# Block decay factors by two small DMAs per block in place of ones-products on TensorE, with a new plan of the instruction order

## The chip, the cores and the metric

The kernel runs on one core of a Trainium2 chip. The metric is the device time of one execution in microseconds (us), the median of several runs. Engines: PE is TensorE (PEld its weight loads), DVE VectorE, ACT ScalarE, POOL GpSimd, SP SyncE, whose queue issues nearly all DMAs here. Lines such as L412 are lines of the kernel that the profile belongs to, so the same function has another number in each kernel.

## The reference

A gated linear attention over 4 x 8 sequences of 768 steps with head size 48, then an MLP with squared rectifier on the 3072 tokens (384 to 2048 to 384):

```python
for t in range(S):
    state = alpha[:, :, t, :, None] * state + np.einsum('bhd,bhe->bhde', k[:, :, t], v[:, :, t])
    y[:, :, t] = np.einsum('bhd,bhde->bhe', q[:, :, t], state)
...
h = x @ w_in
r = np.maximum(h, 0.0)
g = s * (r * r) + b
return g @ w_out
```

`alpha` lies between 0.8 and 1. The kernel cuts the tokens into 24 blocks of 128 (six per batch entry, all heads together). In a block, `b` is the exponential of the running sum of log alpha, the queries are multiplied by `b` and the keys by `1/b`. The state passed to the next block is multiplied by `b` at the block's last step, one factor per head and channel: the *block decay*. The state has channels in partitions, while `b` has time in partitions, so the decay must get from one row (partition 127) into a column.

## The kernel before

The kernel plans itself. Each step is registered with its engine, an assumed duration, a priority and what it reads and writes; a list scheduler then fixes the order of instructions on every engine. On an engine, the ready step with the lowest priority number goes first. SP is planned as an engine too, and executes its queue strictly in that order.

```python
def st_cum(n):                       # PE: running sum, and the sum over the whole block as a column
    la = la_sb[n % 2]
    nc.tensor.matmul(out=cum_ps, lhsT=U_bf, rhs=la[:, :, 0:D], start=True, stop=True)
    if n % NCH == NCH - 1:
        return
    laf = la.rearrange("a h d -> a (h d)")
    for p in range(NP):              # the four ones-products
        nc.tensor.matmul(out=bl_ps[:, p : p + 1], lhsT=laf[:, 128 * p : 128 * p + 128],
                         rhs=ones_col_bf, start=True, stop=True)

def st_exp_b(n):
    nc.scalar.activation(out=b_sb[n % 2], in_=cum_ps, func=AF.Exp)

def st_exp_i(n):
    nc.scalar.activation(out=binv_sb[n % 2], in_=cum_ps, func=AF.Exp, scale=-1.0)
    if n % NCH != NCH - 1:
        nc.scalar.activation(out=blast_sb[n % 2], in_=bl_ps, func=AF.Exp)

def st_snew(n):                      # POOL: new state = (old state + product) * decay
    if n % NCH in (0, NCH - 1):
        return
    bl = blast_sb[n % 2].unsqueeze(2).to_broadcast([128, NP, 96])
    nc.gpsimd.tensor_tensor(out=s_sb[n % 3], in0=t1_sb[n % 2], in1=bl, op=ALU.mult)
# ... cut: for the first block of a sequence st_t1 applies the decay on DVE

def load_op(x, n):                   # the input loads of block n, on SP
    op("SP", TB, loads.index(f"{x}{n}") - 1000, load, n, *SRC[x], w=[(x, n % NIN)], lat=2.0)
```

Five input buffers per operand (`NIN = 5`) let loads run ahead. Blocks 0 to 3 are done in pairs by other code, which the change hardly touches.

## Time and profile before

| | before |
|---|---|
| median of the first three runs | 189.17 us (186.81 to 189.44) |
| span of the profiled core, granted clock | 183.4 us, 1.0 |
| PE / DVE / ACT / POOL busy | 95 / 76 / 58 / 22 % |
| PE from 60 to 180 us | 120.00 us busy of 120 |
| decay ones-products | 64 matmuls (four in each of 16 blocks) |

Busy shares are shares of the whole span.

### The profile page before, as it was taken

To read this page: it belongs to the slowest core of one execution; us is meant where nothing else is said; L and a number is where in the kernel's file an instruction comes from. 1 tells how busy PE (TensorE), PEld (TensorE's weight loads), DVE (VectorE), ACT (ScalarE), POOL (GpSimd) and SP (SyncE) were. 2 spreads that over 40 slices of the span, in tenths; PEclk is the share of its full clock that TensorE was granted. 3 is DMA by queue.
4 is the path that set the end of the run, shared out by engine and by line. 5 is a ranking of instruction groups with operands and counts; after the bars stand their busy time and mean duration, and the time that the engine had idled before them with its cause. 6 is when DMAs were issued, how large, how long until landed. Compare 5 with 4: busy or idle time off the path is not lost.

```text
span 183.4 us, 5324 instructions
## 1 busy us (share of the span) xinstructions
PE 174.6 (95%) x2133; PEld 124.2 (68%) x2135; DVE 138.7 (76%) x255; ACT 106.0 (58%) x215; POOL 40.2 (22%) x70
## 2 busy tenths in 40 slices
PE   6988896999999999999999999999999999999993
PEld 2356574767777776676776776776876776777762
DVE  2377999999899898687789688577897788544421
ACT  3437699946676565674764754853753662665400
POOL 7995032022112423110303311101230131000000
PEclk9999999999999999999999999999999999999999
DMA  5999999999999999996998979996974994101112
GB/s 154 355 295 321 361 370 323 193 178 223 201 185 199 214 183 192 205 211 156 228 169 178 211 153 215 185 228 146 210 175 103 209 194 119 46 4 43 43 43 86
DMA packets 115816, 34.42 MB, mean 188 GB/s; under 512 B 109008, under 2 KB 114256, under 8 KB 115792
## 3 DMA queue, kind: packets, MB, share of 16 engines
q1 hardware_dynamic: 98832, 29.89, 69.2%
q10 hardware_dynamic: 16896, 4.20, 15.7%
q8 instruction: 16, 0.26, 0.6%
q14 instruction: 8, 0.07, 0.1%
q0 software_dynamic: 64, 0.00, 0.0%
HBM read 25.17 MB, written 4.72 MB: 163 GB/s over the span
## 4 chain that ended last, share of the span: by engine, by line
PE 79%; DVE 8%; SPq 6%; DMA 4%; issue 1%; DVEq 0%
PE o_ps L754 32%; PE h_ps L692 31%; PE py_ps L527 5%; SPq L217 5%; PE a_ps L489 4%; DMA gt<-in_k_dram 4%; PE ct_ps L386 2%; DVE colpart L342 2%; DVE gt L707 1%; SPq L309 1%; PE ct_ps L447 1%; PE ct_ps L433 1%; DVE colsum L347 1%; DVE qk L589 1%; PE o_ps L723 1%
## 5 line engine op out<-in xcount | busy, mean ns | idle before, releaser
L692 PE MATMUL h_ps<-xd,w_in_bf 128*128 128x256 bf16 (+1 forms) x624 | 74.4, 265 | 0.1
L701 ACT ACTIVATE r<-h_ps 128x512 bf16<-128x512 f32 x96 | 56.3, 604 | 30.3 <-PE h_ps L692 22.8
L754 PE MATMUL o_ps<-w_out_bf,gt 128*128 128x384 bf16 x368 | 69.5, 326 | 1.4 <-ACT w_out_bf L318 1.3
L692 PEld LDWEIGHTS <-w_in_bf 128*128 128x128 bf16 x624 | 55.1, 97 | 11.1 <-issue 0.4
L707 DVE TENSOR_TENSOR gt<-r 128x512 bf16<-128x512 bf16 x96 | 42.7, 456 | 19.5 <-ACT r L701 18.4
L754 PEld LDWEIGHTS <-gt 128*128 128x128 bf16 x368 | 34.6, 98 | 19.4 <-issue 1.5
L498 DVE TENSOR_TENSOR am<-a_ps,mask 128x1024 bf16<-128x1024 f32 x24 | 29.3, 1221 | 2.3 <-PE a_ps L489 2.0
L483 POOL TENSOR_TENSOR s_st<-s_st,blast 128x384 bf16<-128x384 bf16 x16 | 14.6, 914 | 63.7 <-DVE s_st L472 46.0
L410 POOL CAST vp<-v_in 128x384 bf16<-128x384 f32 x20 | 12.2, 608 | 47.7 <-DMA v_in<-in_v_dram 40.7
L672 ACT ACTIVATE xd<-py_ps 128x384 bf16<-128x384 f32 x22 | 11.0, 502 | 17.8 <-PE py_ps L527 15.9
L765 DVE SCALAR_TENSOR_TENSOR o_sb<-o_ps,s_col,bias_w 128x384 f32<-128x384 f32 x23 | 14.2, 616 | 6.0 <-PE o_ps L754 5.0
L380 ACT ACTIVATE la<-a_in 128x384 bf16<-128x384 f32 x20 | 10.4, 521 | 7.3 <-DVE gt L707 4.5
L416 DVE TENSOR_TENSOR qk<-q_in,b_s 128x384 bf16<-128x384 f32 x20 | 12.5, 627 | 0.8 <-ACT b_s L402 0.7
L421 DVE TENSOR_TENSOR qk<-k_in,binv 128x384 bf16<-128x384 f32 x20 | 11.9, 596 | 0.1
L402 ACT ACTIVATE b_s<-ct_ps 128x384 f32<-128x384 f32 x20 | 9.7, 486 | 2.6 <-PE ct_ps L386 2.2
L405 ACT ACTIVATE binv<-ct_ps 128x384 f32<-128x384 f32 x20 | 9.9, 495 | 0.0
L489 PE MATMUL a_ps<-qkT 64*128 64x128 bf16 x192 | 9.5, 219 | 0.4 <-DVE am L498 0.2
L489 PEld LDWEIGHTS <-qkT 64*128 64x128 bf16 x192 | 5.5, 94 | 6.5 <-issue 5.1
L1026 PE MATMUL o_ps<-zeros 128*128 128x512 bf16 x19 | 7.7, 551 | 1.3 <-DVE zeros L235 1.3
L527 PE MATMUL py_ps<-am,vp 128*32 128x128 bf16 x352 | 8.8, 219 | 0.0
L472 DVE TENSOR_TENSOR s_st<-ct_ps,s_st 64x192 bf16<-64x192 f32 x20 | 7.0, 352 | 2.0 <-PE ct_ps L447 1.6
L527 PEld LDWEIGHTS <-vp 128*32 128x32 bf16 x384 | 6.5, 97 | 0.9 <-issue 0.6
(95 smaller groups left out, 133.4 us busy)
## 6 DMA issues: line engine op xcount, KB each, us to landing
out_dram<-o_sb SPq DMA_DIRECT2D x23, 192.0 KB, 2.5
v_in<-in_v_dram SPq DMA_DIRECT2D x20, 192.0 KB, 3.8
a_in<-in_alpha_dram SPq DMA_DIRECT2D x20, 192.0 KB, 4.1
k_in<-in_k_dram SPq DMA_DIRECT2D x20, 192.0 KB, 4.0
q_in<-in_q_dram SPq DMA_DIRECT2D x20, 192.0 KB, 3.9
wst<-in_moe_w_in_dram SPq DMA_DIRECT2D x4, 768.0 KB, 7.5
gt<-in_moe_w_out_dram SPq DMA_DIRECT2D x4, 768.0 KB, 9.2
gt<-in_alpha_dram SPq DMA_DIRECT2D x2, 384.0 KB, 4.9
```

Of the source, the lines that this page charges most:

```text
L410: nc.gpsimd.tensor_copy(out=vp_sb[n % 4].rearrange("a p (x d) -> a p x d", d=D)[:, :, 0:3:2, :], in_=v_in[n % NIN].rearrange("a (p e) d -> ...
L416: nc.vector.tensor_tensor(out=qk_sb[n % 4][:, 0, :, 0:D], in0=q_in[n % NIN], in1=b_sb[n % 2], op=ALU.mult)
L421: nc.vector.tensor_tensor(out=qk_sb[n % 4][:, 1, :, 0:D], in0=k_in[n % NIN], in1=binv_sb[n % 2], op=ALU.mult,)
L483: nc.gpsimd.tensor_tensor(out=s_sb[n % 3], in0=t1_sb[n % 2], in1=bl, op=ALU.mult)
L489: nc.tensor.matmul(out=a_ps[:, e, p, :], lhsT=qkT[64 * e : 64 * e + 64, 1, p, :], rhs=qkT[64 * e : 64 * e + 64, 0, p, :], start=True, stop ...
L498: nc.vector.tensor_tensor(out=am_sb[n % 2].rearrange("a e p t -> a (e p) t"), in0=a_ps.rearrange("a e p t -> a (e p) t"), in1=(mask2 if n ...
L527: nc.tensor.matmul(out=y_of(n)[32 * (x % 4) : 32 * (x % 4) + 32, x // 4, :], lhsT=(st[:, p, c0 : c0 + 32] if e is None else vp[:, p, c0 + ...
L692: nc.tensor.matmul(out=hp[:, i * n : (i + 1) * n], lhsT=w_in_bf[:, kk, 128 * j : 128 * (j + 1)], rhs=xd_sb[g % 3][:, kk, 0:n], start=(kk = ...
L701: nc.scalar.activation(out=r_sb[w % 2], in_=h_ps[w % 2], func=AF.Relu)
L707: nc.vector.tensor_tensor(out=gt_sb[:, s0 : s0 + m, js[0] : js[0] + len(js)].rearrange("a s j t -> a j s t"), in0=r, in1=r, op=ALU.mult,)
L754: nc.tensor.matmul(out=op[:, 0:d_model], lhsT=gt_sb[:, s0, j], rhs=w_out_bf[:, j, :], start=(j == 0), stop=(j == NJ - 1),)
L765: nc.vector.scalar_tensor_tensor(out=ots, in0=o_ps[(x // 4) % 2][:, 0:d_model], scalar=s_col, in1=bias_w, op0=ALU.mult, op1=ALU.add,)
```

## The change

Intent: take the four ones-products and their small exponential out of every block from the ninth on. The exponential `b` is written so that its last row holds, for each half, the four values of a channel side by side (16 bytes), and two DMAs of 768 bytes spread that row over 48 partitions each. The core of the diff (cut, among others: a new load order, the new values of `P` and of other planning numbers, the wider `blast`, the product that reads `b`, and the plan of the pairs):

```diff
-GROUPS = [2, 2, 1, 1, 2, 2, 2, 2, 2, 2, 2, 2, 2]
+GROUPS = [2, 1, 1, 1, 2, 1, 2, 2, 2, 2, 2, 2, 1, 1, 1, 1]
-NPE = 8
-NAY = 12
+NPE = 9
+NAY = 10
+NBL = 8
+TBL = 0.5
+BLP = -2072
-VC2 = ["ACT", "ACT"]
+VC2 = ["DVE", "DVE"]
 ...
-        if n % NCH == NCH - 1:
+        if n % NCH == NCH - 1 or n >= NBL:
             return
 ...
+    def st_bl(n):
+        row = b_edp(n)[C - 1 : C]
+        for e in range(2):
+            nc.sync.dma_start(
+                out=blast_all[64 * e : 64 * e + D, n % 4, :], in_=row[:, e]
+            )
+
+    def b_edp(n):
+        return b_all[:, n % 2].rearrange("a h d -> a (h d)").rearrange(
+            "a (e d p) -> a e d p", e=2, p=NP
+        )
+
+    def b_of(n):
+        if n < NBL or last_chunk(n):
+            return b_sb[n % 2]
+        return b_edp(n).rearrange("a e d p -> a p e d")
 ...
     def st_exp_b(n):
-        nc.scalar.activation(out=b_sb[n % 2], in_=cum_ps, func=AF.Exp)
+        nc.scalar.activation(out=b_of(n), in_=cum_of(n), func=AF.Exp)
 ...
+            op("ACT", 0.41, t + P["ei"], st_exp_i, n, r=["ct"], w=[("bi", i2)])
+            if not last(n):
+                op("SP", TBL, BLP, st_bl, n, r=[("b", i2)], w=[("bl", s4)], lat=2.0)
```

More of the change, by code (lines that the diff above doesn't have):

```diff
@@ L16 @@
 VW = 144
-GROUPS = [2, 2, 1, 1, 2, 2, 2, 2, 2, 2, 2, 2, 2]
-UNIT = 0.548
-LEAD = {1: 116.8, 2: 316.2, 4: 55.7}
-NPE = 8
-NAY = 12
+GROUPS = [2, 1, 1, 1, 2, 1, 2, 2, 2, 2, 2, 2, 1, 1, 1, 1]
+UNIT = 0.987
+LEAD = {1: 120.0, 2: 301.2, 4: 39.8}
+NPE = 9
+NAY = 10
 RING = 12
@@ L34 @@
 NY = 2
-NKV = 9
+NKV = 8
 NR2 = 2
+NBL = 8
+TBL = 0.5
+BLP = -2072
 TC2 = ["DVE", "DVE"]
-VC2 = ["ACT", "ACT"]
+VC2 = ["DVE", "DVE"]
 CE = ["POOL", "DVE", "ACT", "ACT", "ACT", "ACT", "ACT", "ACT"]
@@ L42 @@
 COLD = 9.0
-P_BM, P_CS, P_BMM = -5, -166.6, 420.9
+P_BM, P_CS, P_BMM = -5, -184.4, 500.0
 P = dict(
-    ln=37.38, cum=-5.89, eb=-21.67, ei=-20.73, vc=52.19, qb=-9.21, kb=4.29, T=47.45,
-    Tc=-10.24, KV=-8.06, t1=-26.76, sn=121.36, Ay=-20.23, A=-31.59, mk=-31.84, y=-27.08,
-    ye=22.77, m1=-10.34, re=8.62, sq=-6.75, m2=-16.59, oe=-37.4, vm=-45.28, ci=-71.74,
-    co=-1313.2, ls=295.04, vn=18.84,
+    ln=30.89, cum=6.75, eb=-15.73, ei=-37.64, vc=58.22, qb=-18.21, kb=1.37, T=51.05,
+    Tc=-26.12, KV=1.1, t1=-18.5, sn=118.41, Ay=-23.07, A=-38.42, mk=-38.49, y=-33.32,
+    ye=38.86, m1=-17.0, re=-0.58, sq=-13.12, m2=-10.9, oe=-38.9, vm=-33.56, ci=-135.11,
+    co=-1083.2, ls=80.19, vn=-135.38,
 )
-LOADS = ["V0", "i0", "A0", "K0", "Q0", "A1", "V1", "Q1", "i1", "K1", "i2", "i3", "v4", "o0", "o1", "o2", "o3", "a4", "k4", "q4"]
+LOADS = ["A0", "V0", "i0", "V1", "A1", "o0", "Q0", "K0", "i1", "K1", "Q1", "i2", "o1", "i3", "v4", "a4", "q4", "o2", "o3", "k4"]
 class Schedule:
@@ L288 @@
     am_sb = many("am", 2, [128, 2, NP, 128], BF16)
-    blast_all = sb.tile([128, 2, NP], BF16, name="blast")
-    blast_sb = [blast_all[:, i] for i in range(2)]
+    blast_all = sb.tile([128, 4, NP], FP32, name="blast")
+    nc.vector.memset(blast_all, 1.0)
+    blast_sb = [blast_all[:, i] for i in range(4)]
     xd_sb = many("xd", 3, [128, 3, 512], BF16)
@@ L399, in st_cum, with last_chunk, cum_of @@
             )
+    def last_chunk(n):
+        return n % NCH == NCH - 1
+    def cum_of(n):
+        return cum_ps if n < NBL or last_chunk(n) else by_pair(cum_ps)
     def st_exp_b(n):
-        nc.scalar.activation(out=b_sb[n % 2], in_=cum_ps, func=AF.Exp)
+        nc.scalar.activation(out=b_of(n), in_=cum_of(n), func=AF.Exp)
     def st_exp_i(n):
         nc.scalar.activation(out=binv_sb[n % 2], in_=cum_ps, func=AF.Exp, scale=-1.0)
-        if n % NCH != NCH - 1:
-            nc.scalar.activation(out=blast_sb[n % 2], in_=bl_ps, func=AF.Exp)
+        if n % NCH != NCH - 1 and n < NBL:
+            nc.scalar.activation(out=blast_sb[n % 4], in_=bl_ps, func=AF.Exp)
+    def st_bl(n):
[12 more added lines that the diff above has]
+        return b_edp(n).rearrange("a e d p -> a p e d")
     def st_vcast(n):
@@ L413, in st_vcast, with by_pair @@
         )
+    def by_pair(x):
+        return x.rearrange("a (p e) d -> a p e d", e=2)
     def st_qb(n):
-        nc.vector.tensor_tensor(
-            out=qk_sb[n % 4][:, 0, :, 0:D], in0=q_in[n % NIN], in1=b_sb[n % 2], op=ALU.mult
-        )
+        out, in0 = qk_sb[n % 4][:, 0, :, 0:D], q_in[n % NIN]
+        b = b_of(n)
+        if len(b.shape) == 4:
+            out, in0 = by_pair(out), by_pair(in0)
+        nc.vector.tensor_tensor(out=out, in0=in0, in1=b, op=ALU.mult)
     def st_kb(n):
@@ L463, in st_t1 @@
     def st_t1(n):
-        bl = blast_sb[n % 2].unsqueeze(2).to_broadcast([128, NP, D])
+        bl = blast_sb[n % 4].unsqueeze(2).to_broadcast([128, NP, D])
         for e in range(2):
@@ L481, in st_snew @@
             return
-        bl = blast_sb[n % 2].unsqueeze(2).to_broadcast([128, NP, 96])
+        bl = blast_sb[n % 4].unsqueeze(2).to_broadcast([128, NP, 96])
         nc.gpsimd.tensor_tensor(out=s_sb[n % 3], in0=t1_sb[n % 2], in1=bl, op=ALU.mult)
@@ L584, in pair_exp_i @@
         )
-        nc.scalar.activation(out=blast_all, in_=bl2_ps, func=AF.Exp)
+        nc.scalar.activation(out=blast_all[:, 2 * m % 4 : 2 * m % 4 + 2], in_=bl2_ps, func=AF.Exp)
     def pair_mul(m, x):
@@ L879, in add_block @@
         op("ACT", 0.45, t + P["ln"], st_ln, n, r=[("a", ii)], w=[("la", i2)])
-        op("PE", 0.27, t + P["cum"], st_cum, n, r=[("la", i2)], w=["ct"], lat=0.16)
+        op("PE", 0.27 if n < NBL and not last(n) else 0.16, t + P["cum"], st_cum, n, r=[("la", i2)], w=["ct"], lat=0.16)
         op("ACT", 0.41, t + P["eb"], st_exp_b, n, r=["ct"], w=[("b", i2)])
-        op("ACT", 0.49, t + P["ei"], st_exp_i, n, r=["ct"], w=[("bi", i2), ("bl", i2)])
+        if n < NBL and not last(n):
+            op("ACT", 0.49, t + P["ei"], st_exp_i, n, r=["ct"], w=[("bi", i2), ("bl", s4)])
+        else:
+            op("ACT", 0.41, t + P["ei"], st_exp_i, n, r=["ct"], w=[("bi", i2)])
+            if not last(n):
+                op("SP", TBL, BLP, st_bl, n, r=[("b", i2)], w=[("bl", s4)], lat=2.0)
         op("POOL", 0.5, t + P["vc"], st_vcast, n, r=[("v", ii)], w=vp, lock=True)
@@ L909, in add_pair @@
         op("ACT", 0.9, t + P["ei"], pair_exp_i, m, r=["a"],
-           w=[("bi", 0), ("bi", 1), ("bl", 0), ("bl", 1)])
+           w=[("bi", 0), ("bi", 1), ("bl", s), ("bl", s + 1)])
         op("DVE", 0.88, t + P["qb"], pair_mul, m, 0, r=[("Q", h), ("b", 0), ("b", 1)], w=qb, lock=True)
@@ L941, in finish_block @@
         if first(n):
-            op("DVE", 0.65, t + P["t1"], st_t1, n, r=[pb(n), ("bl", i2)], w=[("S", i3)])
+            op("DVE", 0.65, t + P["t1"], st_t1, n, r=[pb(n), ("bl", s4)], w=[("S", i3)])
         elif not last(n):
             op("DVE", 0.65, t + P["t1"], st_t1, n, r=[pb(n), ("S", (n - 1) % 3)], w=[("t1", i2)])
-            op("POOL", 0.85, t + P["sn"], st_snew, n, r=[("t1", i2), ("bl", i2)], w=[("S", i3)], lock=True)
+            op("POOL", 0.85, t + P["sn"], st_snew, n, r=[("t1", i2), ("bl", s4)], w=[("S", i3)], lock=True)
         rA, wA = qT, ["a"]
```

## The prediction

> **What bounds the kernel now.** I read the page first, then the busy time by stretch, the chain that ended last, the timeline around single blocks, and the waits of the DMA-issuing queue. The page's first part says that TensorE (PE) is nearly always occupied and VectorE (DVE) is next:
>
> ```profile
> PE 174.6 (95%) x2133; PEld 124.2 (68%) x2135; DVE 138.7 (76%) x255; ACT 106.0 (58%) x215; POOL 40.2 (22%) x70
> ```
>
> Busy PE is not useful PE, so the second view splits the span into stretches (columns: stretch, length, busy us with instruction counts of PE, PEld, DVE, ACT and POOL, granted clock, DMA share, GB/s):
>
> ```profile
> 0.00:40.00 40.00, 34.25 (x372) 22.11 (x375) 31.05 (x54) 27.18 (x42) 17.02 (x38) 1.00 0.99 286
> 40.00:60.00 20.00, 20.00 (x335) 14.80 (x334) 18.86 (x34) 12.90 (x32) 4.39 (x7) 1.00 0.97 203
> 60.00:100.00 40.00, 40.00 (x502) 28.73 (x499) 33.87 (x65) 23.95 (x54) 8.72 (x11) 1.00 1.13 194
> 100.00:140.00 40.00, 40.00 (x481) 29.00 (x469) 31.56 (x59) 23.34 (x53) 7.29 (x10) 1.00 0.88 179
> ```
>
> The reader should see two regimes. From about 38 us to the end PE has no idle time at full clock: there the time is the sum of the PE instructions in the queue. In the first 40 us PE is idle for 5.75 us, and 7.7 us of its busy time are matmuls on zeros that only keep it warm; there loads, casts and the chain of the first block set the pace. The chain that ended last says the same by engine:
>
> ```profile
> PE 79%; DVE 8%; SPq 6%; DMA 4%; issue 1%; DVEq 0%
> ```
>
> So a gain must come out of PE's own work after 38 us, or out of the start. Work saved on ACT, POOL or DVE is worth something only in the start.
>
> Is the long regime already tight? By the spacing of starts, six first-product matmuls of 256 columns cost 0.654 us, four second-product ones 0.65, the masked scores of a block (A) 0.33, its output (y) 0.50, a cumulative sum with ones-products 0.27, the KV product 0.17, a block's transposes 0.44. From 40 to 177.7 us that gives about 490 x 0.109 + 348 x 0.163 + 20 x 0.33 + 20 x 0.50 + 19 x 0.16 + 15 x 0.10 + 16 x 0.17 + 4 x 0.44 = 136 us of 137.7. So 1.6 us are lost there in all, and a new order can win no more than that.
>
> **What the change removes, adds and moves.** The operation in dispute stands in the timeline of PE, once with the four ones-products (65.09) and once in a last chunk, which has none (70.80); columns are start, duration, then the instruction:
>
> ```profile
> 65.09 0.33 PE L386 MATMUL ct_ps<-la,U_bf 128*128 128x384 bf16 x1
> 65.25 0.24 PE L393 MATMUL ct_ps<-ones_col_bf,la 128*128 128x1 bf16 x4
> 65.36 1.47 PE L692 MATMUL h_ps<-xd,w_in_bf 128*128 128x256 bf16 x12
> ...
> 70.80 0.34 PE L386 MATMUL ct_ps<-la,U_bf 128*128 128x384 bf16 x1
> ...
> 70.98 0.81 PE L754 MATMUL o_ps<-w_out_bf,gt 128*128 128x384 bf16 x4
> ```
>
> With ones-products the next matmul starts 0.27 us after the cumulative sum did, without them 0.18. The four cost 0.09 to 0.11 us of PE, not the 0.66 that four times the mean of 165 ns would give: the means are latencies that overlap. The Trainium skill, page "TensorE: Matmul & The Clock Gate", section "Back-to-back issue gap", gives an issue floor of about 25 ns for 1 to 64 columns; 4 x 25 = 100 ns, and the trace agrees.
>
> The sum for PE in the long regime, each an estimate from the spacings above:
> - Ones-products gone for blocks 8 to 22 except the last chunks 11 and 17 (block 23 never had them): 13 blocks x 0.10 = -1.3 us.
> - GROUPS goes from 2 to 8 groups of one block, so 24 units are done as 12 matmuls of 128 columns (0.67 to 0.68 us) in place of 6 of 256 (0.655): 24 x 0.02 = +0.5.
> - NPE 8 to 9: block 8's transposes return from the DMA to PE: +0.44.
> - NAY 12 to 10: A and y go back to back for two more blocks; a switch into this kind of matmul shows about 0.1 us of gap: -0.2.
>
> Together about -0.6 us.
>
> Off PE: ACT loses 13 activations of 128x4 at 0.192 us, 2.5 us in all, of an engine that is 58% busy: nothing by itself. The exponential of the sum is now written with a 16-byte step, and the query product reads it so. The skill, page "SBUF — State Buffer", section on the DMA port swizzle, says that 16-byte lines make each access to a new line pay. No line of this trace shows such an access; if the 0.55 us product (L416) became 0.8, DVE would get 13 x 0.25 = 3 us more over 100 us at 75%, hidden. Four 64-row copies of about 0.5 us move from ACT to DVE in the start, where DVE is 4.8 to 4.9 us busy of every 5 between 20 and 35 us. That hurts a little.
>
> The start has the larger unknown. The first matmul of the MLP begins at 17 us, after a chain (alpha load, log, sum, exponentials, products, transposes, scores, mask, outputs) that the change leaves alone. From 17 to 37.4 us I count 86 x 0.109 + 16 x 0.163 + 3.6 us of attention, 15.6 us of work in 20.4: 4.8 us could be won. The new load order brings the first block of the output weights ahead of the second of the input weights, so its cast and column sums leave the DVE jam at 27 to 36 us, and single groups let block 2 begin its MLP without block 3. Against that: the same 9.4 MB must arrive, and DVE has more copies. I choose -1.2 us.
>
> **The rivals.** First, the decay DMA comes late. For an ordinary block the scaling by the decay (L483, POOL) starts well after the exponential; for the first block of a sequence DVE itself needs the decay (L468) much sooner. Both in the timeline:
>
> ```profile
> 77.70 0.48 ACT L402 ACTIVATE b_s<-ct_ps 128x384 f32<-128x384 f32 x1
> ...
> 78.44 0.20 ACT L407 ACTIVATE blast<-ct_ps 128x4 bf16<-128x4 f32 x1
> ...
> 80.46 0.74 DVE L468 TENSOR_TENSOR s_st<-ct_ps,blast 64x192 bf16<-64x192 f32 x2 [0.38 <-PE ct_ps L447]
> ...
> 83.90 0.48 ACT L402 ACTIVATE b_s<-ct_ps 128x384 f32<-128x384 f32 x1
> ...
> 84.64 0.20 ACT L407 ACTIVATE blast<-ct_ps 128x4 bf16<-128x4 f32 x1
> ...
> 89.04 0.83 POOL L483 TENSOR_TENSOR s_st<-s_st,blast 128x384 bf16<-128x384 bf16 x1 [6.55 <-DVE s_st L472]
> ```
>
> Slack is 89.04 - 84.38 = 4.7 us in the ordinary case and 80.46 - 78.18 = 2.3 us in the other. The page "DMA: Bandwidth & Descriptors", section "Anatomy of one DMA", puts the fixed cost of a DMA near 2 us, mostly the confirmation of the write. The trace brackets it:
>
> ```profile
> v_in<-in_v_dram SPq DMA_DIRECT2D x20, 192.0 KB, 3.8
> out_dram<-o_sb SPq DMA_DIRECT2D x1, 64.0 KB, 1.5
> ```
>
> 1.5 us from issue to landing with nothing else under way, 3.8 behind other loads. With two issues of some 0.4 us I estimate 3 to 5 us. So the ordinary blocks just fit, and the state is needed by the outputs only a block later (some 5.8 us). Blocks 12 and 18 may hold DVE for 1 to 2 us, with PE living on two PSUM banks meanwhile: up to +2 us if the order does not spread them.
>
> Second, the issuing queue becomes the bound. The same page says that a DMA's semaphore wait is spent on the issuing sequencer. The trace agrees; these are the queue's own waits (total us, times, longest):
>
> ```profile
> SPq L777 <- DVE o_sb L765: 32.7, 12, 4.1
> SPq L777 <- DVE gt L707: 28.7, 7, 10.6
> SPq L224 <- ACT r L701: 4.3, 9, 0.7
> ```
>
> 26 more issues at 0.4 us are some 10 us, and each waits for an exponential with loads queued behind it. From 62 to 80 us that queue spends 16 of 18 us issuing[...]. For it: no spare time there. Against it: loads run up to five blocks ahead, and the DMA share falls to 0.46 after 150 us. If true, loads come late, PE gets holes: +2 to +5 us, 190 to 194.
>
> Third, the new order fills the start: up to -4 us, about 184.5. For it stand the 4.8 us; against it, DVE is full exactly there.
>
> **Range and chances.** The median before is 189.17, of 186.81 to 189.44, and the profiled run took 185.12, so single runs scatter by over 1%. -0.6 and -1.2 give 187.4; since two of the four runs before lie well below their median, I take 187.0. One DMA rival at its mild end adds 2.5, a good start takes away 3: 184.2 to 189.8 for 8 in 10. Faster by over 2% needs nearly 4 us, which only the start could give: 0.16. Slower by over 2% needs the queue rival in full: 0.06. Within 2%: 0.78.
>
> **What would show it.** Right: L393 falls from 64 to 12 executions; PE has no idle time after about 37 us; the stretch from the end of the start to the end is about 0.6 us shorter; the tiny DMAs land after 2.5 to 5 us; L483 rarely waits for them. Wrong: waits of L468 or L483 on the decay DMA that pass on to the squares (L707) and make PE idle; POOL or ACT waiting longer for inputs with PE holes behind; the query product well above 0.55 us with DVE above 90% after 60 us; or the first useful 100% slice of PE coming at 33 us or sooner, which would make it faster than I say.

## The result, and the profile after

The changed kernel is correct and takes 204.5 us (203.19 to 207.52, 4 runs) against 188.47 us (186.81 to 189.44, 4 runs) in the same rounds: a ratio of 1.0837 with a 95% interval of 1.0718 to 1.0956. Ratios here are the mean time of one kernel's fast runs over that of the other's fast runs of the same rounds, so they are not quite the ratio of the medians. Executions over 1.5% slower than the fastest of the same kernel are left out of the means. The prediction's range ended at 189.8 us.

First the page of the changed kernel: busy time, and the chain that ended last.

```profile
PE 180.2 (89%) x2242; PEld 127.5 (63%) x2244; DVE 142.0 (71%) x261; ACT 108.2 (54%) x198; POOL 42.3 (21%) x70
...
PE 38%; DMA 24%; DVE 9%; ACT 9%; issue 8%; SPq 6%; POOL 3%; ACTq 0%; POOLq 0%; DVEq 0%
```

PE carried 79% of that chain before and carries 38% now. DMA went from 4% to 24%. Where in time? Busy us by stretch again, for the changed kernel:

```profile
0.00:40.00 40.00, 35.12 (x396) 22.36 (x398) 31.22 (x57) 24.51 (x36) 18.09 (x38) 1.00 0.97 280
40.00:60.00 20.00, 19.78 (x325) 14.74 (x324) 18.57 (x35) 13.16 (x29) 4.28 (x7) 1.00 0.89 182
60.00:180.00 120.00, 107.51 (x1280) 76.60 (x1278) 83.75 (x155) 63.84 (x122) 19.89 (x25) 0.99 0.81 153
```

From 60 us, about where the first decay DMAs stand (57.9 us), to 180 us PE is idle for 12.5 us of 120. Before, it was idle for none. DMA is not busier there: 153 GB/s against 156 before. Who waits tells more. These are the longest waits of the SP queue itself in the changed kernel (total us, times, longest):

```profile
SPq L422 <- ACT b_s L412: 24.4, 8, 5.7
SPq L809 <- DVE gt L739: 19.9, 9, 7.8
SPq L809 <- DVE o_sb L797: 10.3, 5, 5.5
```

L422 is the decay DMA. It waits 24.4 us in all for the exponential, and while it does, everything behind it in the queue stands still. One such case in the timeline of the SP queue (start, duration, instruction):

```profile
85.19 0.77 SPq L227 DMA_DIRECT2D q_in<-in_q_dram  x1
91.74 1.15 SPq L422 DMA_DIRECT2D blast<-b_s  x2
92.93 0.58 SPq L227 DMA_DIRECT2D k_in<-in_k_dram  x1
93.56 0.65 SPq L227 DMA_DIRECT2D v_in<-in_v_dram  x1
```

From 85.96 to 91.74 us the queue issues nothing, although the buffers behind the next two loads show no wait once it moves on. What that does to PE stands in the chain that ended last (start, duration, piece):

```profile
90.91 0.78 ACT b_s L412
91.74 0.51 SPq L422
...
92.30 0.59 SPq L422
...
92.93 0.58 SPq L227
...
93.56 5.36 DMA v_in<-in_v_dram
...
98.98 0.80 POOL vp L437
...
99.82 0.33 PE ct_ps L479 x4
```

Read it downward: the exponential ends, only then are the two decay DMAs issued, only then the k and v loads of the next block; v takes 5.36 us to land, POOL casts it, and PE, which had stood idle for 1.95 us, gets its KV product. The next block's work then leads to the next exponential, which again releases a decay DMA and the loads behind it. The input loads, meant to run blocks ahead, now hang on a computation of the block before.

The small DMAs are not slow: 26 of them, median 1.8 us from issue to landing, where I had estimated 3 to 5. But the other suspect left its mark too. This is what the profile says of the writes and reads of `b` in the changed kernel (durations in ns: shortest/median/longest, of 20 blocks, 13 of them with the new layout):

```profile
L412 ACT ACTIVATE b_s<-ct_ps x20: 484/858/902, 32.1 to 173.3; 128x384 f32<-128x384 f32 x20
L450 DVE TENSOR_TENSOR qk<-q_in,b_s x20: 548/848/1352, 32.6 to 173.9; 128x384 bf16<-128x384 f32 x20
```

The exponential needs 0.86 us for 0.49 and the product 0.85 for 0.55.

### The profile page after: what moved, and what is told of

Same layout as the page of the kernel before. It is cut to its first block, busy times and chain, and to the rows that moved or that the text cites. A ratio compares the mean times of both kernels' runs of the same rounds, so it can differ in the third digit from the quotient of the medians.

```text
span 201.5 us, 5534 instructions
## 1 busy us (share of the span) xinstructions
PE 180.2 (89%) x2242; PEld 127.5 (63%) x2244; DVE 142.0 (71%) x261; ACT 108.2 (54%) x198; POOL 42.3 (21%) x70
## 4 chain that ended last, share of the span: by engine, by line
PE 38%; DMA 24%; DVE 9%; ACT 9%; issue 8%; SPq 6%; POOL 3%; ACTq 0%; POOLq 0%; DVEq 0%
PE o_ps L786 14%; PE h_ps L724 12%; DMA a_in<-in_alpha_dram 9%; DMA v_in<-in_v_dram 9%; SPq L422 3%; DVE am L530 3%; ACT r L733 3%; DMA k_in<-in_k_dram 2%; PE py_ps L559 2%; SPq L227 2%; ACT b_s L412 2%; POOL s_st L515 2%; DMA gt<-in_alpha_dram 2%; DMA blast<-b_s 2%; PE a_ps L521 2%
## 5 line engine op out<-in xcount | busy, mean ns | idle before, releaser
L733 ACT ACTIVATE r<-h_ps 128x512 bf16<-128x512 f32 x96 | 56.0, 601 | 35.2 <-PE h_ps L724 14.6
L786 PE MATMUL o_ps<-w_out_bf,gt 128*128 128x384 bf16 x368 | 71.9, 331 | 0.9 <-ACT w_out_bf L322 0.9
L724 PEld LDWEIGHTS <-w_in_bf 128*128 128x128 bf16 x768 | 59.1, 98 | 16.3 <-issue 6.4
L739 DVE TENSOR_TENSOR gt<-r 128x512 bf16<-128x512 bf16 x96 | 41.4, 444 | 26.1 <-ACT r L733 25.5
L437 POOL CAST vp<-v_in 128x384 bf16<-128x384 f32 x20 | 12.3, 613 | 82.8 <-DMA v_in<-in_v_dram 82.8
L515 POOL TENSOR_TENSOR s_st<-s_st,blast 128x384 bf16<-128x384 bf16 x16 | 16.5, 1033 | 49.5 <-DVE s_st L504 30.0
L450 DVE TENSOR_TENSOR qk<-q_in,b_s 128x384 bf16<-128x384 f32 x20 | 15.8, 792 | 2.0 <-ACT b_s L412 1.5
L412 ACT ACTIVATE b_s<-ct_ps 128x384 f32<-128x384 f32 x20 | 14.8, 742 | 0.0
L1063 PE MATMUL o_ps<-zeros 128*128 128x512 bf16 x28 | 9.5, 495 | 1.5 <-DVE zeros L238 1.3
L390 PE MATMUL ct_ps<-la,U_bf 128*128 128x384 bf16 x20 | 6.7, 336 | 4.0 <-ACT la L384 3.9
L504 DVE TENSOR_TENSOR s_st<-ct_ps,s_st 64x192 bf16<-64x192 f32 x22 | 7.8, 354 | 2.6 <-PE ct_ps L479 2.2
```

What stands on the lines that cost most here:

```text
L412: nc.scalar.activation(out=b_of(n), in_=cum_of(n), func=AF.Exp)
L437: nc.gpsimd.tensor_copy(out=vp_sb[n % 4].rearrange("a p (x d) -> a p x d", d=D)[:, :, 0:3:2, :], in_=v_in[n % NIN].rearrange("a (p e) d -> ...
L450: nc.vector.tensor_tensor(out=out, in0=in0, in1=b, op=ALU.mult)
L724: nc.tensor.matmul(out=hp[:, i * n : (i + 1) * n], lhsT=w_in_bf[:, kk, 128 * j : 128 * (j + 1)], rhs=xd_sb[g % 3][:, kk, 0:n], start=(kk = ...
L733: nc.scalar.activation(out=r_sb[w % 2], in_=h_ps[w % 2], func=AF.Relu)
L739: nc.vector.tensor_tensor(out=gt_sb[:, s0 : s0 + m, js[0] : js[0] + len(js)].rearrange("a s j t -> a j s t"), in0=r, in1=r, op=ALU.mult,)
```

## The experiments

Theory A: the decay DMA, placed ahead of loads in the in-order SP queue, holds them up until its exponential is done. Rival B: the 16-byte steps of `b` slow ACT and DVE, and PE with them. Rival C: the issues, traffic and latency of the 26 DMAs. Rival D: the new order itself. Eighteen runs were made, in five calls; all ratios are to the kernel before on the same chip in the same call (its medians there: 186.05, 186.29, 188.35, 187.24 and 186.12 us). The medians in the table are of all runs of a kernel, the ratios of the fast ones alone. Runs of different calls are compared by ratio only.

| run | what is left of the change | median us | ratio (95% interval) |
|---|---|---|---|
| e1_ones_back | new order only | 187.11 | 1.0064 (1.0000 to 1.0128) |
| e16_ones_again | the same again | 187.59 | 1.0070 (1.0030 to 1.0109) |
| e5_constant_dense | order, DMAs without wait | 187.69 | 1.0079 (1.0009 to 1.0149) |
| e13_act_steps | order, steps on ACT alone | 188.05 | 1.0054 (1.0013 to 1.0094) |
| e14_dve_steps | order, steps on DVE alone | 187.99 | 1.0064 (1.0019 to 1.0110) |
| e6_strided_ones | order, steps on both | 189.44 | 1.0195 (1.0123 to 1.0266) |
| e17_strided_again | the same again | 189.48 | 1.0182 (1.0141 to 1.0223) |
| e3_constant_row | order, steps, DMAs without wait | 189.69 | 1.0210 (1.0153 to 1.0266) |
| e7_late_issue | all, DMAs later in the queue | 190.60 | 1.0217 (1.0137 to 1.0297) |
| e4_dense_exp | all but the steps | 196.32 | 1.0550 (1.0468 to 1.0632) |
| e2_act_queue | all, DMAs issued by ACT | 196.26 | 1.0572 (1.0507 to 1.0637) |
| e9_changed_again | all | 204.31 | 1.0961 (1.0853 to 1.1068) |
| e8_old_order_dma | old parameters, planned anew with the DMAs | 206.28 | 1.1063 (1.0980 to 1.1145) |
| e15_loads_first | all, DMAs planned behind the loads | 226.95 | 1.2155 (1.2082 to 1.2227) |
| e12_old_kv | old order, DMAs at the KV product, POOL copy | 192.38 | 1.0159 (1.0063 to 1.0255) |
| e18_old_kv_strided | old order, DMAs at the KV product, steps | 189.21 | 1.0167 (1.0125 to 1.0210) |
| e10_late_pool_row | new order, late DMAs, POOL copy | 194.16 | 1.0270 (1.0164 to 1.0376) |
| e11_old_reader | old order, DMAs at the reader, POOL copy | 193.83 | 1.0325 (1.0244 to 1.0406) |

Unless it says otherwise, a run keeps the instruction order of the changed kernel on every engine. Runs whose decay or scaling is wrong are marked so below; e4, e13 and e14 passed the comparison with the reference all the same, so that comparison does not see a mixing of channels of similar size. e3 and e5, with a constant 0.5, failed it.

### First call: undo the mechanism, move the queue, take away the wait, take away the steps

e1_ones_back, against D (`cum_of`, which then returns `cum_ps`, is cut):

```diff
 def st_cum(n):
-        if n % NCH == NCH - 1 or n >= NBL:
+        if n % NCH == NCH - 1:
 def st_exp_i(n):
-        if n % NCH != NCH - 1 and n < NBL:
+        if n % NCH != NCH - 1:
 def st_bl(n):
+        return
 def b_of(n):
-        if n < NBL or last_chunk(n):
+        if True:
```

> The changed kernel in its exact order, but the decays come from the ones-products again and the exponential is written densely: no decay DMA. If the decay DMA path (its wait on the issuing queue, its traffic or its strided exponential) makes the loss, the time is that of before, 186 to 190 us, with no idle PE from 60 us on. If the new order itself is bad, it stays at 200 us or more.

187.11 us, ratio 1.0064. The new order without the DMAs costs 0.6%, not 8%. D explains only that.

e2_act_queue:

```diff
-            nc.sync.dma_start(
+            nc.scalar.dma_start(
```

> The same two small DMAs per block, issued by ACT in place of SP, all orders else the same. Theory (a decay DMA that waits for its exponential holds up the input loads behind it on the SP queue): the holes of PE go, 187 to 192 us, the waits of POOL and ACT for loads fall to the level of before (some 41 us for v_in). Rival (strided exponential, or the DMA traffic and latency themselves): stays at 200 to 206 us.

196.26 us, ratio 1.0572: neither number. The loads are free again (POOL waits 47.1 us for v, near the 40.7 of before, and not 82.8), but ACT now pays. Its timeline in this run:

```profile
66.22 0.51 ACTq L422 DMA_DIRECT2D blast<-b_s  x1
66.39 0.61 ACT L733 ACTIVATE r<-h_ps 128x512 bf16<-128x512 f32 x1
66.78 0.60 ACTq L422 DMA_DIRECT2D blast<-b_s  x1
67.42 1.72 ACTq L470 DMA_TRANSPOSE qkT<-qk  x1
69.19 1.08 ACT L733 ACTIVATE r<-h_ps 128x512 bf16<-128x512 f32 x2 [2.19 <-DMA blast<-b_s]
```

Two issues and the transpose's issue (1.72 us) fill ACT's sequencer until 69.14 us, and ACT is idle for 2.19 us before the rectifiers (L733), which empty PE's two PSUM banks. So the expectation of "187 to 192" was wrong: another queue is no gift where its engine has to serve PE. How much of the 5.7% is ACT's issuing was not taken apart; POOL also waits 19.7 us for the decay in this run.

e3_constant_row (wrong result):

```diff
+    ones_row = sb.tile([128, H, D], FP32, name="ones_row")
+    nc.vector.memset(ones_row, 0.5)
 def st_bl(n):
-        row = b_edp(n)[C - 1 : C]
+        row = ones_row.rearrange("a h d -> a (h d)").rearrange("a (e d p) -> a e d p", e=2, p=NP)[C - 1 : C]
```

> Wrong result on purpose: the small DMAs stay on the SP queue but read a constant row, so they have no exponential to wait for. Theory (waiting on the queue): 187 to 192 us. Rival (issue time and traffic of 26 small DMAs, or the strided exponential): stays at 200 to 206 us. The issues still cost 13 x 1.16 = 15 us of the SP queue here.

189.69 us, ratio 1.021. Same DMAs, same queue, same places; only the reason to wait is gone, and with it 6.3 points of the 8.4 (1.0837 - 1.0210; the two ratios are of different calls, and against e9 below it is 7.5). PE's stretch in this run:

```profile
60.00:180.00 120.00, 117.94 (x1480) 85.98 (x1479) 90.88 (x167) 70.56 (x134) 17.84 (x25) 1.00 0.84 156
```

2.1 us idle, where the changed kernel has 12.5. This is A's prediction, and neither B nor C can make it.

e4_dense_exp (wrong decays):

```diff
 def cum_of(n):
-        return cum_ps if n < NBL or last_chunk(n) else by_pair(cum_ps)
+        return cum_ps
 def b_of(n):
-        if n < NBL or last_chunk(n):
+        if True:
```

> Wrong result on purpose: the exponential is written densely, as before, and the small DMAs read the same 768 bytes of its last row in the wrong order. Same DMAs, same waits, no 16-byte steps. If the steps (exponential 0.88 us for 0.49, product 0.86 for 0.55) make the loss: 187 to 192 us. If the queue does: 198 to 204 us, a little less than the changed kernel because the exponential ends 0.4 us sooner.

196.32 us, ratio 1.055: 2 us below the range for the queue, and above that for the steps. The queue still loses most, but the steps cost 2.9 points (1.0837 - 1.0550) when the wait is there. An exponential that ends 0.4 us sooner also releases the queue sooner; no run shows how much of the 2.9 that is.

### Second call: split the remaining 2.1%, and move the DMAs without falsifying them

e5_constant_dense (wrong result) joins the edits of e3 and e4:

> Wrong result on purpose: constant row as in e3_constant_row and the dense exponential as in e4_dense_exp, so only issue time, traffic and latency of the 26 small DMAs are left. If the 1.5% between e3_constant_row and e1_ones_back are the 16-byte steps: 186.5 to 188 us (ratio near 1.005). If they are the issues on the SP queue: as e3_constant_row, 189 to 190 us (ratio near 1.02).

187.69 us, ratio 1.0079: within the interval of the ones-products in the same order (1.0064). Issue time, traffic and latency of the DMAs cost nothing that shows, and the removal of the ones-products gains nothing that shows. C falls, as far as these intervals see.

e6_strided_ones is e1 with the change's `cum_of` and `b_of` put back:

> Ones-products and no small DMA, as in e1_ones_back, but the exponential keeps its 16-byte steps: the price of the steps alone. 13 x 0.4 us more on ACT and 13 x 0.3 us more on DVE, neither of which is full: if they stay hidden, 186.5 to 188 us (ratio near 1.006); if they delay the rectifiers that PE waits for, 188.5 to 191 us (ratio 1.015 to 1.03).

189.44 us, ratio 1.0195: the steps are not hidden, though neither engine is full. It agrees with e3 against e5 (1.021 against 1.008). And e3, with the small DMAs, but not their wait, in place of the ones-products, is at 1.0210: a second pair that shows no cost of C.

e7_late_issue, correct, one thing moved (the loop around these lines is cut):

```diff
+                if name == "st_bl":
+                    held[args[0]] = i
+                    continue
+                if name == "st_snew" or (name == "st_t1" and args[0] % 6 == 0):
+                    if args[0] in held:
+                        order.append(held.pop(args[0]))
+                order.append(i)
```

> The changed kernel with one thing moved: each pair of small DMAs stands in the SP queue just ahead of the instruction that needs the decay, behind the 2 to 7 transfers that it used to hold up. Correct result. Theory (order within the SP queue): loads go out without waiting for an exponential, 188 to 193 us, unless the decay now comes late for POOL and the state (then 193 to 200 us, with POOL waiting for the decay DMA). Rival (cost of the DMAs themselves): 200 to 206 us.

190.6 us, ratio 1.0217, as good as taking the wait away altogether (1.0210). PE, ACT, DVE and POOL keep their order; only the place of the small DMAs in the SP queue differs. POOL does wait for the decay now:

```profile
POOL s_st L527 <- DMA blast<-b_s: 31.8, 7, 6.8
```

This is 31.8 us of waiting that costs nothing that shows; POOL's product is not needed until the next block's outputs. A is confirmed with a correct kernel: the loss hung on the place in the queue.

e8_old_order_dma: the change, with every planning number of before (groups, priorities, load order), planned anew:

> The groups, priorities and load order of before, with the decay DMAs of the change from block 8 on. If the loss belongs to the mechanism and not to the new order: 194 to 205 us. If the old order, which loads further ahead of its exponentials, does not expose the wait: 185 to 189 us, at best 1.3 us below before.

206.28 us, ratio 1.1063. The mechanism loses with the old planning numbers too, and not less (its interval overlaps that of e9 below). The hope that the old plan loads far enough ahead was wrong: its SP queue, planned anew with the small DMAs first, waits at them for ACT's exponentials 36.0 us in twelve stops (18.5 us in seven put down to `b`, 17.5 in five to `1/b`).

### Third call: candidates

e9_changed_again is the changed kernel without an edit:

> The changed kernel once more, as a control on the same chip as the three candidates: 202 to 206 us, ratio 1.075 to 1.095.

204.31 us, ratio 1.0961, so just above the expected 1.095. The loss in ratio varies by a point between chips and calls.

The three candidates keep `b` dense; POOL copies its last 32 rows into the layout that the DMAs need:

```diff
+    def st_row(n):
+        r = slice(C - 32, C)
+        nc.gpsimd.tensor_copy(
+            out=row_edp(n)[r].rearrange("a e d p -> a p e d"),
+            in_=b_sb[n % 2][r].rearrange("a (p e) d -> a p e d", e=2),
+        )
```

e10_late_pool_row adds it to e7:

> Candidate in the new order, correct: late issue as in e7_late_issue, and the exponential stays dense because POOL copies its last 32 rows into the order that the small DMAs need. If both costs add up as found (wait and steps), what is left is e5_constant_dense: 186.5 to 188.5 us, ratio 1.004 to 1.012. If the copy queues behind POOL's own waits for v loads and the decay comes late: ratio 1.02 or more.

Ratio 1.027, the worse of the two cases, from two fast runs.

e11_old_reader and e12_old_kv use the exact order of the kernel before on every engine, with `st_bl(n)` called at the head of `st_snew`/`st_t1` or of `st_KV`:

> Candidate in the order of before: no ones-products from block 8 on, dense exponential, POOL copies the last rows, the two small DMAs issued just ahead of the instruction that needs the decay. If the 1.3 us of PE that the change wanted are real and nothing else is lost: ratio 0.992 to 0.998. If the late decay makes the state late: ratio above 1.005 and POOL waiting for the decay DMA.

> As e11_old_reader, with the small DMAs issued a little earlier, where the KV product is issued: more time for the decay to land, more chance to hold up loads. Ratio 0.992 to 0.998 if neither bites; above e11_old_reader if the queue order matters more than the landing.

1.0325 and 1.0159. In e11 POOL waits 24.8 us for exponentials before its copies, which stand in order among its other work, and then 17.3 us for the decay; POOL is busy for 53.7 us instead of 40.2. Issued earlier (e12) it is 1.7 points lower, though the two intervals just overlap. Neither beats the kernel before.

### Fourth call: which steps, and the planner's own priority

e13_act_steps and e14_dve_steps (both wrong) are e6 with only the write or only the read in steps:

```diff
 # e13: st_qb
-        b = b_of(n)
+        b = b_sb[n % 2]
 # e14: st_exp_b
-        nc.scalar.activation(out=b_of(n), in_=cum_of(n), func=AF.Exp)
+        nc.scalar.activation(out=b_sb[n % 2], in_=cum_ps, func=AF.Exp)
```

> Wrong result on purpose: e6_strided_ones with the product reading the exponential as if it were dense, so only the writes of ACT have 16-byte steps (13 x 0.4 us). If the 1.3% between e6_strided_ones and e1_ones_back are ACT's: ratio near 1.02; if they are DVE's: near 1.006.

> Wrong result on purpose: the reverse, a dense exponential and a product of DVE that reads it in 16-byte steps (13 x 0.3 us). If the 1.3% are DVE's: ratio near 1.02; if ACT's: near 1.006.

1.0054 and 1.0064: neither alone costs anything that shows over e1 (1.0064 in another call). Both expectations had assumed that one of them would.

e15_loads_first:

```diff
-BLP = -2072
+BLP = -500
```

> The changed kernel with one number changed: the planned priority of the small DMAs is put behind the loads, so the plan issues every load that its buffers allow ahead of them; the plan is made anew, so the order of the other engines moves too. Theory (loads held up behind a wait): 188 to 194 us. If the loads' distance ahead does not matter: 200 us or more.

226.95 us, ratio 1.2155: the opposite of the expected gain, so "loads first" is not the cure by itself. In its SP queue:

```profile
82.83 1.83 SPq L227 DMA_DIRECT2D v_in<-in_v_dram  x2
84.71 7.86 SPq L422 DMA_DIRECT2D blast<-b_s  x6
```

Six small DMAs, the decays of three blocks, stand behind all the loads that the five buffers allowed and are only issued from 84.71 us on. The changed kernel issued its first at 57.9 us. The state comes late, and PE runs dry from the other side:

```profile
60.00:100.00 40.00, 23.12 (x246) 15.10 (x245) 18.33 (x33) 11.71 (x24) 4.25 (x7) 0.77 0.87 178
```

23 us busy of 40. Part of the loss is then the granted clock, 0.77 here. In an in-order queue both sides can starve: too early, the DMA holds up the loads; too late, the loads hold up the DMA. e7 sits between.

### Fifth call: the steps once more, and the old order without POOL's copies

> e1_ones_back once more, beside e17 on the same chip: ratio 1.003 to 1.010. It is the base for the price of the steps.

> e6_strided_ones once more, beside e16. If the 16-byte steps of ACT and of DVE cost 1.3% only when both are there, the ratio is 1.016 to 1.023 as before; if e6 read high by chance, it is within 0.4% of e16, 1.003 to 1.012.

1.0070 and 1.0182 side by side (one run of e16 took 431 us and is outside the fast runs). The intervals do not touch: the steps do cost 1.1% when both are there, and nothing that shows (e13, e14) when one is.

e18_old_kv_strided is e12 with the steps of the change in place of POOL's copy:

> The exact order of before on every engine, with the strided exponential and the small DMAs of the change, issued where the KV product is issued, and no copy on POOL. If the loss of e12_old_kv is POOL's copies: ratio 0.995 to 1.005. If it is the decay coming late or the loads held up again: 1.01 or more.

1.0167, no better than e12. That does not clear POOL's copies: this run has the steps in their place, which cost 1.1% in e16 and e17. Whether steps here and copies there lose the time, or one common cause such as the decay's lateness, stays open.

## Why the prediction was wrong

**What held.** In the kernel before PE's queue sets the end from 40 us on, and the ones-products fell from 64 to 12. That L515 rarely waits for the decay held in its count (3 waits, 9.8 us). One sign of being wrong came as it was written: POOL waits 82.8 us for v where it waited 40.7, with holes of PE behind.

**The step that failed: the second rival.** The prediction put it as "26 more issues at 0.4 us are some 10 us, and each waits for an exponential with loads queued behind it", named the right queue, sized it at +2 to +5 us and gave it 0.06, "against it: loads run up to five blocks ahead". Measured, the wait is worth 6.3 to 7.5 points of ratio, some 12 to 14 us of 188 (e3 and e7 against the changed kernel and e9). Two things were mis-sized. Issue time was counted, which shows no cost (e5 against e1, e3 against e6). And five buffers were taken for five blocks of lead. The trace of the kernel before already denied that. One v load and the cast that takes it (block 13, found by pairing loads and casts in order):

```profile
77.96 0.66 SPq L224 DMA_DIRECT2D v_in<-in_v_dram  x1
...
81.99 0.51 POOL L410 CAST vp<-v_in 128x384 bf16<-128x384 f32 x1 [4.75 <-DMA v_in<-in_v_dram]
```

From block 8 on its v loads are issued a median of 4.3 us before their cast (3.3 to 6.5), the k loads 8.6 us before their product, while the exponentials of `b` start a median of 6.4 us apart: half a block to two blocks of lead, not five. In the changed kernel the k loads are down to 6.8 us.

The queue's order decides how far loads really run ahead: the diff gave the small DMAs priority -2072 and the loads about -1000, and in the planned queue of the changed kernel the k and v loads of a block regularly stand behind the decay DMA of a block just ahead of it. So, in the chain shown above, the wait closes a loop of exponential, decay DMA, load, landing, cast, product, next exponential. The two priorities in the diff would have raised the question but not settled it: the plan starts a step only when its inputs are done there, so the plan itself has no such wait. It comes when the exponential on the chip ends after the queue has reached the small DMA.

Two readings of the prediction were also off, neither of which moves the result: its sum for PE from 40 us on gives 135.8 us, so 1.9 us and not 1.6 were lost there; and from 62 to 80 us the issues of the SP queue add up to 13.5 us, not 16, so some time was spare.

**The step called hidden.** "DVE would get 13 x 0.25 = 3 us more over 100 us at 75%, hidden" was wrong in two ways. The product's size was right (0.85 us), but the write of ACT, which grew by 0.37 us, was left out; and together they cost 1.1% (e16, e17), with the same again in the pair e3 and e5. From 60 to 180 us PE is idle for some 1.4 us in e6 and in e17, for 0.5 in e13 and in e14, and for 0.2 in e1. Write and read follow one another on the way from sum to query product. That this is why only both together cost something is my reading; no run shows it.

**The term for the start.** "I choose -1.2 us" had the wrong sign. With the new order and nothing else (e1), the first 40 us hold this much of the MLP:

```profile
L725 PE MATMUL h_ps<-xd,w_in_bf 128*128 128x256 bf16 x48 | 6.1, 272 | 1.0 <-ACT w_in_bf L322 1.0
L725 PE MATMUL h_ps<-xd,w_in_bf 128*128 128x128 bf16 x60 | 4.0, 219 | 0.1
L787 PE MATMUL o_ps<-w_out_bf,gt 128*128 128x384 bf16 x16 | 3.3, 326 | 1.4 <-ACT w_out_bf L322 1.4
```

60 matmuls of 128 columns are worth 30 of 256, so this is 78 and 16; before, it was 90 and 20. At the spacings of the prediction that is 12 x 0.109 + 4 x 0.163 = 2.0 us behind, an estimate of the sign of the 0.6 to 0.7% (1.2 us) of e1 and e16, and above it.

**The first rival** (the decay DMA late) hardly happened in the changed kernel: the DMAs land after 1.8 us once issued, and POOL waits for them three times. It happened in e7, without harm that shows, and in e15, ruinously.

**The gain that was sought.** The 1.3 us of PE from the ones-products shows in no pair: e5, which has the DMAs with dense `b` and no wait, is not below e1. If it is there, it is smaller than the intervals of some 0.7%.

In sum: new order +0.7 and steps +1.1 to 1.3 points; the rest of the measured 8.4, some 6.3, is the wait (7.5 against e9). The parts depend on each other: with a dense `b` the wait is worth 4.7 points (e4 less e5). No version was found that beats the kernel before.

## What to carry to other kernels

A transfer that waits for a computation does not belong ahead of prefetches in an in-order queue: look where it stands in the queue and what stands behind it, before counting its bytes or its issue time. The number of buffers does not say how far loads run ahead; the order in the issuing queue does. And a dependent transfer can be moved towards its reader until the reader waits a little for it (e7: POOL's 31.8 us of waiting cost nothing that shows), but moved behind all loads it starves instead (e15).

## What the Trainium skill lacked or had wrong

- "DMA: Bandwidth & Descriptors", section "Anatomy of one DMA", says that a DMA's semaphore wait happens on the issuing sequencer, and that the fixed cost is near 2 us; it gives the second for DMAs issued by GpSimd, while those here, and those that the prediction applied it to, are issued by SP. Both agree here all the same (24.4 us of such waits; 1.8 us for 768 bytes within SBUF). What it lacks is the consequence: the wait also stops unrelated transfers behind it, here for up to 5.7 us at a time and 6.3 to 7.5 points of ratio.
- The same page, section "Issuing engines are not separate DMA queues", calls the time to initiate a DMA usually small relative to the DMA. For these small ones it is 0.58 us of issue for 1.8 us to landing. On ACT (e2) two such issues and a transpose's of 1.72 us left the engine idle for 2.19 us at one stop.
- "SBUF — State Buffer", section on the DMA port swizzle, says that accesses which cross 16-byte lines pay, without a size. The trace agrees: here 384 fp32 values per partition at 16-byte steps cost ACT 0.37 us more per write (0.86 for 0.49) and DVE 0.30 us more per read (0.85 for 0.55), about 0.8 to 1 ns per value.
